# A written-out instruction order for all five engines, replaced by another one

## The chip, the cores and the metric

The kernel runs on one core of a Trainium2 chip. The metric is the device time of one execution in microseconds (us), the median of three runs. Besides the runs there is one execution recorded by the hardware profiler; every duration below is from its trace.

## The reference

The kernel computes one layer of an E-Branchformer (a speech encoder) and the gradients of its eight inputs from a given gradient of its output. Sizes: batch B = 2, T = 4000 tokens, D = 144 channels, taps K = 5, all in bf16.

```
xa   = layernorm(x)
q, k, v = split(xa @ w_qkv)
p    = softmax(q @ k^T * D**-0.5)            # 4000 x 4000 for each batch
glob = (p @ v) @ w_att_out
u, g = split(gelu(xa @ w_mlp_in))
gc   = depthwise_conv(layernorm(g), dw_csgu)  # 5 taps over time
loc  = (u * gc) @ w_mlp_out
m    = concat(glob, loc)
m    = m + depthwise_conv(m, dw_merge)
out  = x + m @ w_merge
return out, and the vjp of out for grad_out: dx and seven weight gradients
```

## The kernel before

**Tiling.** Each batch is cut into 32 tiles of 125 tokens. For each batch `phase_att` (L936) walks over its tiles and makes the forward and the backward of attention in one pass, while units of the local branch (`local_units`, L480: 5-tap convolution, GELU and their gradients) are worked in between. `Merge` (L1391) follows with the merge convolution, the output and dx, and `Final` (L1595) with the weight gradients. `Head` (L127) makes products of weights at the start.

**One tile of attention.** The names in italics are the short names of the text.

- *quad* (q0 to q3; L1028 and L1034): eight matmuls into PSUM (`ps`), 500 keys wide, for scores S of this tile and for dP of the tile before. L1034 adds the last 16 of the 144 channels.
- DVE takes a row statistic and copies (L1052), ACT makes the exponentials (L1060). P lies in `Pb`.
- SP issues the DMA transpose of P (`SX<-Pb`, L1064, *pt*). The two *y halves* (y0, y1; L1084) multiply the result with the layer-normed input into the one PSUM tile `yz`.
- dS is made from dP and P: ACT cast (L1073) and DVE product (L1075), or DVE alone (L1070). SP issues its DMA transpose in two halves (`SX<-SX`, L1256, *st0*, *st1*); the two *z halves* (z0, z1; L1131) multiply those.
- Small work on DVE, ACT and POOL after y (L1091 to L1113) and z (L1135) makes the operands of the next steps. SP issues the transposes of those too: `zt<-qz` (L1145, *zt*), `dhT<-dhr` of the local branch (L650, *dhT*), and `qt<-qz` (L1010, *jt*), which brings the query side of a later quad.
- *X groups* (x0 to x5; L1176): the gradients of keys and values, up to 16 matmuls each into a PSUM tile, which DVE adds to `acc` (L1180, L1182).
- *jm* (L988 to L992) is the projection of a later tile's queries; *t_unit*, *gc_unit*, *dgn*, *dug* are groups of the local branch (L597, L608, L623, L560).

The last two tiles of a batch use transposes on PE (L1121) in place of the DMA. With a `d` or `t` behind it, as in `st1t`, a name means the end of the first or the second batch.

**Fillers.** 126 matmuls of `warm` (L154) at the start and 50 (L1966) between the batches compute nothing that is used; they are part of PE's list like all others.

**The order.** The program is first emitted in the order of the code, and `Planner.grouped` (L898) collects it into 7014 groups: up to 16 matmuls of one PSUM tile (a quad is one group) on PE, one instruction on every other engine. `Planner.plan` (L924) then gives each engine the order that a table, `ORDER` (L723), holds as differences of group numbers, by chaining each instruction to the one before it without a semaphore:

```
    for e, order in ORDER.items():
        ...
        for g in order:
            for i in groups[g]["ins"]:
                if prev is not None:
                    self.tc.add_manual_dep(i, prev.name, ...NoSync...)
```

Each engine runs its list strictly in order: an instruction that waits for data holds all behind it. SP's list holds nearly all DMA issues, loads and stores as well as transposes. PE has 1799 groups, DVE 2394, ACT 1350, POOL 916 and SP 555.

**The ends.** At the end of the first batch and of the second, SP's list holds loads for the merge (`open_early`, L1402: `go_h`, `Yg`; `late_y`, L1427; `late_w`, L1443) beside the last transposes; `Hmm` (L1451, groups H0 to H15, L1459) needs them. The quads and outputs of the merge are L1556 to L1560. In the final stretch `dwm` (L1765) is a chain: a product into `pg` (L1773), five steps on DVE (L1780 to L1784), a transpose on PE (`fpt`, L1790), an ACT copy (L1793) and stores (L1786, L1795), once for 128 channels and once for 16.

Of the kernel before, what the change touches and what calls it, by code (L numbers as in the profile page):

```python
# [723 lines left out]
for _s in """  # L724
PE 10 1 1 1 1 1 1 1 1 1 1 1 1 1 1 1 1 1 1 1 1 1 1 1 1 1 1 1 1 1 1 185 -184 187 -186 1 1 1 1 1 1 1 1 1 1 1 1 1 1 1 1 173 2 11 -185 1 1 1 1 1 1 1 1 1 1
 198 -197 1 198 -197 1 1 1 1 1 1 195 -194 1 1 1 1 1 192 -191 1 1 1 1 1 1 1 1 1 1 1 1 209 2 62 -58 60 -57 -217 1 1 1 232 2 -233 1 1 1 1 1 1 276 -36 2
 24 -265 1 1 1 1 285 -21 2 2 71 14 -352 272 2 2 85 -83 2 2 83 -74 2 2 -294 1 295 2 -296 1 297 2 2 2 -302 304 5 -308 1 1 1 1 1 1 1 304 -303 1 305 -304
 1 311 -310 1 310 -309 1 309 10 35 11 -43 2 73 -70 6 91 -3 -86 22 69 -65 2 8 2 65 -62 2 13 9 73 -71 13 32 19 -16 4 10 23 -9 13 -17 29 -10 14 1 -7 24
 -6 34 -32 39 -25 32 -28 2 48 -46 3 5 14 6 14 2 18 -44 46 -14 1 17 10 18 -7 -2 10 9 -5 2 20 -13 2 9 6 1 24 -6 2 10 5 17 -7 -2 10 8 -4 8 2 2 11 -9 3 10
 1 -7 21 6 -4 38 -28 6 15 -2 14 4 -2 -6 12 5 11 -2 18 -12 1 13 4 13 5 13 -7 8 -10 20 -6 2 8 13 -8 6 6 12 -11 13 4 14 2 7 11 -2 14 3 -8 12 -11 22 -2 18  # L730
 -12 14 1 11 -25 30 -12 16 3 18 -7 -9 2 15 -11 1 16 -2 6 17 -15 7 6 18 -12 14 -13 31 -14 18 16 -7 -3 1 10 4 10 -8 12 8 2 18 2 -16 1 26 -7 10 4 17 -7
 -2 10 10 -6 2 8 14 -2 18 2 -14 16 -15 19 9 8 17 -7 -2 14 5 4 -13 18 7 -2 18 -12 1 13 4 6 3 2 19 -17 3 21 -17 8 14 6 -4 -6 14 14 -2 18 2 1 -15 1 24 -6
 36 -25 8 10 8 -10 14 5 4 5 3 2 16 -12 14 1 -14 24 -6 13 4 23 -9 2 12 1 -5 7 4 3 5 10 -2 18 -12 1 13 4 9 19 -9 2 12 -4 5 3 4 2 5 9 -6 2 8 -6 18 -11 14
 2 10 -6 33 -20 4 9 -2 14 9 -13 17 3 7 -2 18 -12 20 -19 21 4 9 19 -9 2 12 -4 7 4 2 3 9 -2 18 -12 1 13 4 6 13 17 -12 5 -2 10 9 -5 9 2 13 -2 6 12 -11 13
 5 -4 16 4 18 -7 -6 14 10 -20 14 2 22 -20 6 2 3 13 1 -7 18 2 11 -6 12 -16 28 12 -7 -2 14 2 -6 10 6 13 -2 -16 22 1 11 6 -4 15 18 -13 6 -2 14 -4 10 -4 8
 6 -5 13 -2 25 -19 1 24 -4 11 27 -7 -18 7 19 7 -17 14 18 -11 9 6 13 -12 14 4 6 5 3 21 -17 10 -8 2 4 10 10 -6 2 8 13 -8 6 6 12 -11 13 19 -18 4 16 25
 -18 9 2 12 7 -4 -7 20 2 16 -12 1 13 1 4 7 3 4 21 -7 -7 5 14 4 -8 12 14 -4 2 18 -12 1 13 13 -9 17 20 -9 2 12 -4 6 4 5 11 -6 3 7 12 -11 -7 24 -4 10 31
 -29 2 4 16 -11 9 14 5 -9 13 11 -8 5 7 12 8 -26 7 21 4 10 4 11 7 1 10 -24 4 14 27 -25 2 27 -21 2 5 8 7 21 -7 2 12 -11 38 -7 8 -24 5 28 -19 14 22 -13 3
 14 -9 10 18 -25 40 -22 2 1 12 -2 10 6 -2 6 4 4 -6 7 11 34 -32 1 46 -4 -6 2 2 10 -3 5 2 2 2 1 2 2 27 -25 27 -26 28 26 4 -28 32 -30 2 1 7 2 2 2 7 -5 2
 7 -3 4 4 -1 5 4 -6 4 4 -7 4 5 -1 4 -1 2 23 -1 4 1 -7 10 1 11 1 10 1 11 -41 52 12 -22 11 12 -61 12 59 12 -11 22 9 -80 89 -77 49 11 9 -58 12 63 9 9 -70  # L740
 44 -32 11 51 -21 25 -46 30 18 -9 -30 9 25 7 -3 5 2 -5 2 -24 9 20 -16 13 5 2 -5 2 200 1 1 1 1 1 1 -219 220 1 1 1 -182 -26 28 -26 207 1 1 1 1 1 -172 2
 171 1 1 1 1 -171 172 1 1 1 1 -174 175 1 1 1 -176 177 1 1 1 1 1 1 1 1 1 -175 2 4 2 168 1 1 1 1 1 1 -172 2 4 2 2 2 161 1 -160 2 1 169 -168 1 171 5 1 2
 1 4 3 -2 3 3 3 7 -28 50 -7 19 -18 2 1 6 1 2 1 23 -20 5 1 18 -16 1 21 3 1 -3 39 -32 1 41 -39 6 -5 8 4 42 -33 3 -2 3 33 1 16 -26 35 14 7 -17 28 -26 16
 -14 44 -40 14 2 8 14 6 1 11 2 4 6 5 8 2 7 5 4 4 2 3 -17 26 -2 20 2 -16 1 19 13 2 18 -9 2 12 -4 8 4 4 2 7 -5 3 18 2 10 -24 1 30 -13 17 14 2 12 6 -4 -7
 1 20 -7 5 6 12 -11 19 2 4 9 19 -7 -2 10 7 -3 7 14 -12 3 7 6 12 -11 13 10 6 -12 24 12 -7 -2 10 6 -2 6 5 11 4 1 -7 20 7 -5 16 -15 35 -15 8 8 -10 19 -5
 2 22 -15 2 17 -15 2 14 -11 4 25 -7 2 14 -13 19 23 -10 1 2 8 4 4 -2 6 5 11 -2 6 12 -11 17 -4 15 18 -7 -3 11 -10 19 -5 2 7 15 -13 7 4 20 2 -16 1 33 -14
 18 15 -7 -2 14 10 -8 -6 28 -10 8 6 1 11 2 4 9 22 -18 11 8 -14 24 -20 14 2 22 -20 6 2 3 13 -6 18 4 -15 21 -4 19 17 -12 5 -2 10 9 -5 9 2 13 -2 18 -12 1
# [1304 lines left out]
```

## Time and profile before

| | us |
|---|---|
| runs | 1248.24, 1252.67, 1252.02; median 1252.02 |
| profiled execution | 1248.45 |
| its span | 1246.7 |
| TensorE busy (PE) | 1202.6 |
| VectorE busy (DVE) | 1053.6 |
| ScalarE busy (ACT) | 739.3 |
| GpSimd busy (POOL) | 444.9 |

The span runs from the first to the last instruction of the trace; the profiled execution is 1.75 us longer. The mean granted clock of TensorE is 0.993. "PE" is matmuls, "PEld" weight loads that run beside them, "SPq" the time that SP's sequencer takes to issue a DMA. A wait is written with the engine and line that waits, and behind the arrow with what ended the wait. Roughly, the span is: head to 50 us, attention of the first batch to 550, the merge of the first batch to 650, attention of the second batch to 1150, the merge and the weight gradients to the end.

### The profile page before, as it was taken

The numbers are of one execution on the slowest core, as the hardware profiler recorded it, in microseconds if no ns is written. First come the engines' busy times: TensorE is split into PE (matmuls) and PEld (weight loads), VectorE is DVE, ScalarE is ACT, GpSimd is POOL, SyncE is SP. The second block draws the span as 40 slices with busy tenths as digits, with TensorE's granted clock in tenths as the row PEclk, the third lists the DMA queues.
The fourth block names the chain that finished last, engine by engine and source line by source line (L and its number), as shares of the span: only waits on it lengthen the run. The fifth ranks groups of instructions, "written<-read, shape, count | busy, mean of one in ns | idle before, by whom it ended". The sixth has DMA issues, their size and how long they took to land.

```text
span 1246.7 us, 38759 instructions
## 1 busy us (share of the span) xinstructions
PE 1202.6 (96%) x15890; PEld 947.8 (76%) x15890; DVE 1053.6 (85%) x2862; ACT 739.3 (59%) x1183; POOL 444.9 (36%) x920
## 2 busy tenths in 40 slices
PE   9999999999999999999999999999999999999997
PEld 7667777777777777789876777777777777677996
DVE  8688989898989888879769898989888989877665
ACT  5866555656565656544746656666656666554273
POOL 8444333433333333213534433333334333222020
PEclk9899999999999999999999999999999999999998
DMA  3579999898989999985249889999898999999332
GB/s 106 121 133 155 161 154 162 155 166 156 169 153 165 150 160 160 163 201 156 66 103 158 159 162 161 156 166 152 147 174 157 159 159 170 169 171 188 95 101 69
DMA packets 638399, 186.52 MB, mean 150 GB/s; under 512 B 621025, under 2 KB 633164, under 8 KB 638214
## 3 DMA queue, kind: packets, MB, share of 16 engines
q1 hardware_dynamic: 616664, 176.66, 79.6%
q10 hardware_dynamic: 21348, 7.13, 2.9%
q8 instruction: 124, 2.03, 0.7%
q14 instruction: 55, 0.45, 0.1%
q0 software_dynamic: 208, 0.25, 0.1%
HBM read 20.82 MB, written 14.22 MB: 28 GB/s over the span
## 4 chain that ended last, share of the span: by engine, by line
PE 62%; DVE 15%; DMA 14%; ACT 6%; issue 2%; SPq 1%; POOL 1%; ACTq 0%; DVEq 0%; POOLq 0%
PE X L1176 14%; PE ps L1028 11%; PE yz L1131 8%; DMA SX<-SX 6%; PE yz L1084 5%; PE ps L1034 5%; DMA SX<-Pb 4%; DVE Pb L1052 4%; PE Hps L1459 3%; PE po L1556 3%; ACT Pb L1060 2%; DVE acc L1182 2%; DVE SX L1075 2%; DMA qt<-qz 1%; PE warm L154 1%
## 5 line engine op out<-in xcount | busy, mean ns | idle before, releaser
L1052 DVE TENSOR_SCALAR_CACHE_REDUCE Pb<-ps 125x1000 bf16<-125x1000 f32 x256 | 306.0, 1196 | 68.7 <-PE ps L1034 66.1
L1060 ACT ACTIVATE Pb<-Pb,nm 125x1000 bf16<-125x1000 bf16 x256 | 277.4, 1127 | 120.8 <-DVE nm L1054 119.9
L1176 PE MATMUL X<-SX 125*128 125x144 bf16 x2048 | 294.5, 227 | 2.0 <-DVE acc L1180 0.7
L1176 PE MATMUL X<-SX,Pb 125*128 125x144 bf16 x2048 | 293.8, 226 | 0.0
L1073 ACT CAST SX<-ps 125x1000 bf16<-125x1000 f32 x189 | 187.9, 994 | 161.5 <-PE ps L1034 159.9
L1028 PE MATMUL ps<-xaT_m,qt 128*128 128x500 bf16 x1024 | 262.2, 376 | 8.7 <-DVE Pb L1052 5.2
L1182 DVE TENSOR_TENSOR acc<-X,acc 125x432 f32<-125x432 f32 x372 | 201.2, 550 | 30.6 <-PE X L1176 29.6
L1176 PEld LDWEIGHTS <-SX 125*128 125x128 bf16 x2048 | 197.3, 97 | 28.9 <-issue 27.7
L1176 PEld LDWEIGHTS <-Pb 125*128 125x128 bf16 x2048 | 200.2, 98 | 3.7 <-issue 3.1
L1131 PE MATMUL yz<-xa_aug,SX 125*128 125x144 bf16 x2048 | 151.6, 229 | 11.6 <-DMA SX<-SX 9.5
L1084 PE MATMUL yz<-xa_aug,SX 125*128 125x145 bf16 x2048 | 145.7, 227 | 4.1 <-DMA SX<-Pb 4.1
L1131 PEld LDWEIGHTS <-SX 125*128 125x128 bf16 x2048 | 132.8, 98 | 20.7 <-DMA SX<-SX 13.8
L1028 PEld LDWEIGHTS <-qt 128*128 128x128 bf16 x1024 | 91.0, 98 | 71.1 <-issue 8.4
L1084 PEld LDWEIGHTS <-SX 125*128 125x128 bf16 x2048 | 132.6, 98 | 6.7 <-DMA SX<-Pb 5.6
L1075 DVE TENSOR_TENSOR SX<-SX,Pb 125x1024 bf16<-125x1024 bf16 x189 | 131.2, 698 | 7.4 <-ACT SX L1073 5.0
L1034 PEld LDWEIGHTS <-qt 16*128 16x128 bf16 x1024 | 26.6, 91 | 111.3 <-issue 111.3
L1034 PE MATMUL ps<-XR,qt 16*128 16x500 bf16 x1016 | 102.1, 382 | 0.0
L1070 DVE TENSOR_TENSOR SX<-ps,Pb 125x1000 bf16<-125x1000 f32 x67 | 80.1, 1195 | 2.5 <-PE ps L1034 1.9
L638 POOL TENSOR_SCALAR l_w<-gdr,nc,c 125x144 f32<-125x144 bf16 x64 | 30.5, 481 | 94.2 <-DVE c L636 84.5
L533 POOL TENSOR_SCALAR l_a<-l_sq 125x576 bf16<-125x576 bf16 x32 | 23.2, 725 | 111.7 <-ACT l_sq L531 107.2
L1109 POOL TENSOR_SCALAR SX<-qz,rl 125x144 bf16<-125x144 bf16 x62 | 25.1, 405 | 95.0 <-DVE rl L1091 84.3
L1004 POOL COPY qz<-qz 125x64 bf16<-125x64 bf16 (+1 forms) x124 | 34.0, 292 | 67.9 <-ACT qz L994 67.1
(475 smaller groups left out, 2141.6 us busy)
## 6 DMA issues: line engine op xcount, KB each, us to landing
go_h<-in_grad_out_dram SPq DMA_DIRECT2D x4, 567.0 KB
Yg<-ug_d SPq DMA_DIRECT2D x4, 567.0 KB
Yn_d<-yn ACTq DMA_DIRECT2D x64, 35.2 KB
Zn_d<-qz ACTq DMA_DIRECT2D x64, 35.2 KB
ug_d<-ugr ACTq DMA_DIRECT2D x32, 70.3 KB
SX<-in_x_dram SPq DMA_DIRECT2D x16, 140.6 KB
out_dram<-Pb SPq DMA_DIRECT2D x16, 140.6 KB
out_dram<-SX SPq DMA_DIRECT2D x16, 140.6 KB
```

Source lines behind the costliest of these rows:

```text
L1028: mm = nc.tensor.matmul(pp[r // 2][:, r % 2, 0:CH], QT[i][:, 3 * h, :], xaTm[:, c * CH:(c + 1) * CH], start=True, stop=False)
L1034: nc.tensor.matmul(pp[r // 2][:, r % 2, 0:CH], QT[i][rs, 1 + h, :], xr, start=False, stop=True)
L1052: nc.vector.tensor_scalar(pv(Pbuf, i % NPB, c2), src, -1.0, 3.0e38, op0=ALU.mult, op1=ALU.min, accum_out=NM[i][:, c2:c2 + 1])
L1060: nc.scalar.activation(v, v, ACT.Exp, bias=NM[i][:, 4:5], scale=-1.0)
L1070: nc.vector.tensor_tensor(pv(Sbuf, i % NDB, c2), src, pv(Pbuf, i % NPB, c2), op=ALU.mult)
L1073: nc.scalar.copy(pv(Sbuf, i % NDB, c2), src)
L1075: nc.vector.tensor_tensor(sc, sc, pchunk(i % NPB, c2), op=ALU.mult)
L1084: nc.tensor.matmul(Y, PT[0:PB, j, :], xaa[:, j, 0:D + 1], start=(j == 0), stop=(j == NB - 1))
L1131: nc.tensor.matmul(Z, ST[0:PB, j, :], xaa[:, j, 0:D], start=(j == 0), stop=(j == NB - 1))
L1176: nc.tensor.matmul(X[:, jj, :], l, r, start=(n_ == 0), stop=(n_ == len(ops) - 1))
L1182: nc.vector.tensor_tensor(av, X[0:PB, 0:nj, :], av, op=ALU.add)
L1459: nc.tensor.matmul(H[a // 6][0:rows, a // 3 % 2, (a % 3) * D:(a % 3 + 1) * D], lhs, self.src[h][:, 2 + j, :], start=(j == 0 and a % 3 == 0 ...
```

## The change

The table `ORDER` is replaced by another, made from durations that were read from a trace. The groups, their instructions, operands, buffers and semaphores are the same; only the order in each engine's list differs.

```diff
 ORDER = {}
 for _s in """
-PE 10 1 1 1 1 1 1 1 1 1 1 1 1 1 1 1 1 1 1 1 1 1 1 1 1 1 1 1 1 1 1 185 -184 187 -186 1 1 1 1 1 1 1 1 1 1 1 1 1 1 1 1 173 2 11 -185 1 1 1 1 1 1 1 1 1 1
...
+PE 10 1 1 1 1 1 1 1 1 1 1 1 1 1 1 1 1 1 1 1 1 1 1 1 1 1 1 1 1 1 1 1 1 1 1 1 1 1 1 1 1 1 1 1 1 1 1 1 1 1 1 1 1 1 1 1 1 1 1 1 1 1 1 1 1 1 1 1 1 1 146
...
 """.strip().replace("\n ", " ").split("\n"):
```

(The lines of all five engines change in this way.) Decoded, the two tables compare like this. In attention most groups stand within a place or two of where they stood:

| engine | entries | at the same place | median of places moved | most |
|---|---|---|---|---|
| PE | 1799 | 789 | 1 | 49 |
| DVE | 2394 | 463 | 2 | 103 |
| ACT | 1350 | 206 | 2 | 52 |
| POOL | 916 | 190 | 2 | 43 |
| SP | 555 | 129 | 1 | 94 |

Places of which the text speaks, with the start that each group has in the trace of before:

| place | list before | list of the change |
|---|---|---|
| PE, head | 31 fillers, `hps` (7.83), ..., first quad (19.55) at place 99 | 70 fillers, `hps`, ..., first quad at place 114 |
| PE, attention (one example) | jm 1107.01, z0 1109.17, q1 1110.20, dgn 1111.46, x0 1111.78, x1 1112.53, q2 1113.28 | jm, q1, dgn, x0, x1, z0, q2 with x2 ahead of it |
| SP, attention (one example) | pt 1110.20, jt 1115.15, st0 1116.48, st1, pt, dhT 1129.80, zt 1131.71 | pt, jt, zt, st0, st1, pt, dhT |
| PE, 576 to 612 | H groups, then 50 fillers among transposes of the second batch's input | up to 34 of the fillers stand earlier, among the H groups |
| SP, 1133 to 1165 | st0t 1132.99, zt 1134.85, two loads, st1t 1138.14, then 14 loads and more | st0t, eight loads, zt, six loads, st1t |
| POOL, 1135 to 1143 | clears of `Yg` at 1141.85 and 1142.52 behind L1111 to L1113 | the same clears 14 and 15 places earlier |
| PE, tail | `pg` of 16 channels 1230.09, quads of the output, transposes and products 1233.46 to 1235.76 (six groups), last `pg` 1235.99 | last `pg` ahead of those six groups |

In the second row from the top the count of X groups that stand earlier and of z, y and q groups that stand later is the main regularity of PE's list; in SP's list it is a zt that stands ahead of an st (42 times in the two attention stretches).

6 lines of the change are left out of this document (3 added, 3 removed), and 277 rows, old and new, of the table ORDER.

## The prediction

> **What bounds the kernel now.** I read the page's engine totals first, then its chain of waits, then the stretches of the span, then what TensorE waited for.
>
> ```profile
> span 1246.7 us, 38759 instructions
> PE 1202.6 (96%) x15890; PEld 947.8 (76%) x15890; DVE 1053.6 (85%) x2862; ACT 739.3 (59%) x1183; POOL 444.9 (36%) x920
> PE 62%; DVE 15%; DMA 14%; ACT 6%; issue 2%; SPq 1%; POOL 1%; ACTq 0%; DVEq 0%; POOLq 0%
> ```
>
> TensorE is busy for 1202.6 of 1246.7 us, so at most 44.1 us of recorded idle time can go; no matmul is removed. The chain that ends last runs through PE for 62%, and through DVE and DMA for 15% and 14%: where PE is not the one that works, it waits for an eviction or a transpose. The profiled execution took 1248.45 us, 1.75 us more than its span. It lies near the lowest of the three runs (1248.24) and 3.57 us under their median (1252.02).
>
> ```profile
> 0.00:25.00 25.00, 23.57 (x185) 19.66 (x185) 20.64 (x85) 13.12 (x35) 21.66 (x48) 1.00 0.43 113
> 25.00:50.00 25.00, 24.94 (x245) 15.15 (x243) 17.25 (x32) 19.87 (x40) 11.76 (x49) 0.89 0.39 96
> 100.00:550.00 450.00, 439.63 (x5846) 337.20 (x5846) 399.13 (x1023) 272.52 (x412) 158.58 (x330) 1.00 0.94 160
> 550.00:600.00 50.00, 49.95 (x802) 49.67 (x800) 42.02 (x182) 24.38 (x35) 15.89 (x21) 1.00 0.56 146
> 600.00:650.00 50.00, 47.25 (x618) 40.35 (x616) 35.76 (x88) 28.82 (x54) 22.53 (x38) 1.00 0.38 92
> 650.00:1150.00 500.00, 483.87 (x6394) 371.19 (x6392) 438.53 (x1116) 303.87 (x457) 177.41 (x373) 1.00 0.95 162
> 1225.00:1246.70 21.70, 13.41 (x152) 9.91 (x150) 13.82 (x71) 4.41 (x17) 1.93 (x2) 0.82 0.26 72
> ```
>
> The columns are the stretch, its length, busy time of PE, PE weight load, DVE, ACT and POOL, PE's granted clock, the DMA share and GB/s. The two attention stretches hold 10.4 and 16.1 us of PE's idle time, and their DMA share is 0.94 and 0.95. The last stretch holds 8.3 us, 600 to 650 holds 2.75. What the change can win is therefore in attention and in the last 21.7 us.
>
> ```profile
> PE yz L1131 <- DMA SX<-SX: 9.5, 11, 2.6
> PE ps L1028 <- DVE Pb L1052: 5.2, 11, 1.7
> PE fpt L1790 <- DVE Pb L1788: 4.6, 2, 2.4
> PE yz L1084 <- DMA SX<-Pb: 4.1, 7, 0.9
> PE ps L1028 <- DMA qt<-qz: 3.1, 5, 0.9
> ```
>
> Waits of PE: total, times, longest. Three of the five are DMA transposes that land late: dS^T before a z half (9.5), P^T before a y half (4.1) and q^T before a score quad (3.1), together **16.7 us**.
>
> **The change part by part.** Work and buffers stay; only who stands ahead of whom in each of the five queues moves. So nothing is added to the 1202.6 us, and each part is worth only what it does to waits.
>
> *Attention, PE's queue.* Comparing the two lists, I see one systematic move: X groups (L1176) go ahead of y, z and q groups. Of the 118 z groups 50 stand behind at least 0.3 us more PE work than before, of the 119 y groups 36, of the 228 quads 42; the mean is 0.47 us for z0, 0.86 for z1, 0.33 for y and 0.37 for q0.
>
> ```profile
> 1107.19 0.47 PE L992 MATMUL pj<-VUT,goT 128*125 128x144 bf16 x5
> 1109.17 1.19 PE L1131 MATMUL yz<-xa_aug,SX 125*128 125x144 bf16 x16 [1.50 <-DMA SX<-SX]
> 1110.20 1.01 PE L1028 MATMUL ps<-xaT_m,qt 128*128 128x500 bf16 x4
> 1111.46 0.30 PE L623 MATMUL pd<-eb,gT 128*128 128x68 bf16 x4
> 1111.78 0.22 PE L1176 MATMUL X<-SX 125*128 125x144 bf16 x1
> 1113.28 1.01 PE L1028 MATMUL ps<-xaT_m,qt 128*128 128x500 bf16 x4
> 1090.60 1.19 PE L1131 MATMUL yz<-xa_aug,SX 125*128 125x144 bf16 x16 [2.63 <-DMA SX<-SX]
> ```
>
> At 1109.17 a z half waits 1.50 us for its transpose. In the new list the quad and the three groups behind it (1110.20 to the next quad at 1113.28: 3.08 us) stand ahead of it, which is more than the wait. At 1090.60, the longest wait (2.63), PE's list is unchanged. The X groups that move forward are ready: of 154 that go ahead by over 0.3 us one alone would wait, for 0.2 us, by the ends of its producers in this trace.
>
> *Attention, SP's queue.* Every transpose is issued by SP, in order, and an issue is not short:
>
> ```profile
> L1145 SPq DMA_TRANSPOSE zt<-qz x60: 1177/1254/2346, 83.6 to 1134.9; - x60
> L650 SPq DMA_TRANSPOSE dhT<-dhr x32: 1222/1282/2625, 151.4 to 1129.8; - x32
> L1256 SPq DMA_TRANSPOSE SX<-SX x124: 1558/2324/4082, 49.9 to 1138.1; - x124
> L1064 SPq DMA_TRANSPOSE SX<-Pb x62: 4724/5220/6641, 36.1 to 1124.3; - x62
> ```
>
> These are ns (min, median, max). The new list puts a zt ahead of a dS^T transpose 42 times, at a median of 1.25 us of SP each. I walked SP's new list with the readiness and the issue durations of this trace: the dS^T transposes are issued 0.7 us later on average (P^T 0.13), because a zt or dhT now stands in front of them. That takes back what the X groups give: set against PE's new list, the lead of a landing over its z half changes by -0.09 (z0) and +0.21 (z1) us, over y0 by +0.13, over a quad by +0.18. Some leads get longer (1109.17: 3.08 more work less an issue 1.23 later, enough for its 1.50), others fall short: 27 of some 246 landings, by 28.0 us together, of which 5.8 are one case below. Readiness is itself a result of the old order, so for an item moved forward this walk shows it too late: the 28.0 is an upper end. **I take 0** for attention: the mean lead hardly moves. Bounds: -16.7 (all three waits gone) to +22.2 (28.0 less 5.8, each a wait).
>
> The Trainium skill, page "DMA: Bandwidth & Descriptors", section "Issuing engines are not separate DMA queues", says that the sequencer's time to start a DMA is usually small beside the DMA itself. By that rule a zt ahead of a dS^T would cost nothing, the shortfalls would mostly vanish, and the sum would go to its lower bound. The rows speak against it here: 1.25 and 2.32 us of SP per issue are not small beside waits of 0.9 to 2.6.
>
> *DVE, ACT and POOL in attention.* Median moves of two places, in queues that are 0.89 or less busy. DVE's score statistics are the one wait of PE on them (5.2 us in the rows above). A promoted DVE item that isn't ready holds what is behind it, and the quads wait for that; a quad that comes 0.37 us later gives the same back. I take 0; bounds -5.2 and +5.2, the same row both ways.
>
> *Head.* All 126 warm fillers stay, but 70 instead of 31 stand ahead of the first real group.
>
> ```profile
> 7.83 0.22 PE L194 MATMUL hps<-ident,Pb 128*128 128x128 bf16 x1
> 9.03 2.31 PE L154 MATMUL warm<-SX 128*125 128x290 bf16 x17
> 11.18 0.41 PE L220 MATMUL hps<-SX 128*128 128x144 bf16 x4
> 19.55 0.59 PE L1028 MATMUL ps<-xaT_m,qt 128*128 128x500 bf16 x2
> ```
>
> A filler takes (11.18 - 9.03) / 17 = 0.126 us, so the group of 7.83 comes 39 x 0.126 = 4.9 us later. The first quad (19.55) has 15 more places ahead, all fillers: +1.9 us. By 44 us both lists have done the same work, and PE has no idle time in 25 to 50, so the delay is paid only as far as later steps hang on the first quad. I take +1.9, bounds 0 and +4.9.
>
> *Between the batches.* Up to 34 of the 50 second fillers go from 595-612 into 576-594, where PE had no idle time, and H groups and transposes come 3 to 4 us later. The cover is then missing where PE waits for the layer norm:
>
> ```profile
> 594.75 1.02 PE L1966 MATMUL warm<-VUT,ident 128*125 128x288 bf16 x7
> 606.80 0.60 PE L410 MATMUL pt<-ident,go_r 125*80 125x125 bf16 x8 [1.28 <-DVE R L411]
> ```
>
> At the head's 0.126 us each, 34 of them are 4.3 us: an upper end if all that they hid comes out. The H groups that fill in instead are the same work, and the wait that shows is 1.28, so I take +1.0, bounds 0 and +4.3.
>
> *End of batch two.* The last dS^T transpose goes 15 places back on SP, behind loads for the merge.
>
> ```profile
> 1138.14 2.84 SPq L1256 DMA_TRANSPOSE SX<-SX  x1
> 1144.62 1.19 PE L1131 MATMUL yz<-xa_aug,SX 125*128 125x144 bf16 x16
> ```
>
> SP's walk issues it 11.5 us later, its z half has 3.9 us more work ahead and 1.8 us of slack: the 5.8 us short. Part of the walk's delay is a load that waits for a POOL memset, which the new POOL list does 15 places earlier; without it the shortfall is near 0. I take half, +2.9; bounds 0 and +5.8. The Trainium skill, page "TensorE: Matmul & The Clock Gate", section "HAM oscillation", says that PE gaps beyond about 3.4 us throttle the clock; an estimate by it is some 1.7 us more if the wait comes out whole. The sum leaves it out.
>
> *Tail.*
>
> ```profile
> 1233.46 0.17 PE L1790 MATMUL fpt<-ident,Pb 16*5 16x16 bf16 x1
> 1233.56 0.49 PE L1615 MATMUL fpt<-ident,Pb 128*128 128x128 bf16 x4
> 1233.99 0.28 PE L1556 MATMUL po<-SX 128*125 128x144 bf16 x1
> 1234.55 0.51 PE L1625 MATMUL fpt<-goT,Pb 128*128 128x144 bf16 x4
> 1235.99 0.79 PE L1773 MATMUL pg<-Pb,xaT_m 128*128 128x432 bf16 x4
> 1239.15 0.27 PE L1790 MATMUL fpt<-ident,Pb 128*5 128x128 bf16 x1 [2.38 <-DVE Pb L1788]
> ```
>
> The last dependent chain is pg at 1235.99, five DVE steps, a transpose, pg again, DVE again, and the last store. Its list is unchanged, but it begins six PE places earlier: the transposes and products of 1233.46 to 1233.99 (0.53 us), of 1234.55 and of the same line just ahead of pg (some 0.44 each, their 0.51 less the overlap) now come behind it. That is -1.4 us, bounds -8.3 (the stretch's idle time) and 0.
>
> **Sum** against 1248.45: 0 + 0 + 1.9 + 1.0 + 2.9 - 1.4 = +4.4, so 1252.9; rounded, **1253 us**, beside the median of 1252.02. A difference under about 0.5% (6.3 us) can't be told from no change here.
>
> **The rivals.** *Faster: X groups cover the transposes.* The transposes' producers are moved forward as well, the shortfalls vanish, and the 16.7 us of DMA waits go: 1248.45 - 16.7 + 4.4 = 1236. For it: the move of X groups is aimed at exactly those waits, and X groups are ready. Against: SP's own issues come 0.7 us later, and DMA is already 0.94 busy. *Slower: SP's order decides.* The zt and dhT issues ahead of dS^T make z halves late; half of the 22.2 us bound is 11.1: 1248.45 + 4.4 + 11.1 = 1264; all of it is 1275. It decides once more than some 6 us of the 22.2 turn into waits. For it: 42 x 1.25 us; against: z halves stand 0.47 to 0.86 us later too. *The order is not kept*: each engine runs its queue in program order, so I give this nothing of its own.
>
> **How the numbers follow.** Forecast 0.37 (1246 to 1258), faster rival 0.28, slower rival 0.35. The range takes in the slower rival's whole size and the faster rival with most of the tail's bound (1236 - 6.9 = 1229): 1230 to 1275. Faster by over 0.5% 0.28, within 0.37, slower 0.35.
>
> **What would show it.** PE's waits for dS^T and P^T should stay near 13.6 us with other places; the wait at 1109 should be gone. A total under 5 is the faster rival, over 20 the slower. The first quad should start near 21.5 us, the last z half behind its transpose near 1150 should wait up to 5.8 us, and the last pg chain should begin 1.4 us nearer to the end. I am wrong if DVE or POOL becomes what PE waits for in attention, or if the busy time of PE itself moves.

## The result and the profile after

The changed kernel takes **1242.17 us** (median of seven runs, 1238.75 to 1245.96), the kernel before 1248.85 us beside it (seven runs, 1248.24 to 1252.67). The ratio is **0.9941, with an interval of 0.9922 to 0.9959**: some 7 us, or 0.59%, faster. The forecast was no measurable difference, 1253 us. The profiled execution of the changed kernel took 1242.5 us.

The first rows are from the page of the changed kernel: its span, the engine totals, and the chain that ended last by engine.

```profile
span 1240.7 us, 38869 instructions
PE 1198.4 (97%) x15890; PEld 950.0 (77%) x15890; DVE 1058.6 (85%) x2862; ACT 740.1 (60%) x1183; POOL 461.4 (37%) x920
PE 61%; DVE 16%; DMA 12%; ACT 4%; POOL 4%; issue 3%; ACTq 0%; SPq 0%; DVEq 0%; POOLq 0%
```

PE's matmuls are as many as before, the span is 6.0 us shorter, and the chain of waits has the same make: PE for 61%, then DVE and DMA. Nothing else became the bound. The stretches of the span show where PE's idle time went, and a row of 5 us shows the place that the end of the second batch pays for. The columns are those of the prediction's rows.

```profile
100.00:550.00 450.00, 442.28 (x5914) 342.36 (x5912) 400.30 (x1032) 272.52 (x410) 163.87 (x331) 1.00 0.98 166
550.00:600.00 50.00, 46.44 (x700) 45.74 (x699) 47.47 (x192) 27.32 (x45) 24.25 (x30) 0.96 0.30 84
650.00:1150.00 500.00, 482.44 (x6344) 369.48 (x6342) 438.80 (x1105) 301.23 (x452) 185.81 (x371) 1.00 0.96 163
1140.00:1145.00 5.00, 1.14 (x17) 0.79 (x15) 1.25 (x3) 0.99 (x1) 0.00 (x0) 1.00 1.22 175
1225.00:1240.70 15.70, 10.11 (x124) 7.70 (x121) 10.16 (x53) 2.45 (x11) 0.00 (x0) 0.89 0.21 59
```

The first batch's attention (100 to 550) now has 7.7 us of PE idle instead of 10.4. The merge behind it (550 to 600) has 3.6 instead of 0.05, and in the five microseconds from 1140 on PE works for 1.14. The last stretch has 5.6 us of PE idle where before had 8.3. So the change wins and loses at the same time, by stage. What PE waited for, over the whole span (total, times, longest):

```profile
PE yz L1085 <- DMA SX<-Pb: 6.6, 9, 1.8
PE yz L1132 <- DMA SX<-SX: 6.2, 8, 1.4
PE ps L1029 <- DVE Pb L1053: 4.7, 14, 0.8
PE pt L410 <- DVE R L450: 3.3, 1, 3.3
PE Hps L1460 <- issue: 2.9, 1, 2.9
PE fpt L1791 <- DVE Pb L1789: 2.8, 2, 2.1
PE Hps L1460 <- DMA Pb<-in_x_dram: 2.1, 1, 2.1
```

(Lines stand one further down than before.) The waits for P^T, dS^T and q^T, 16.7 us before, are 12.8 here: neither gone nor grown. Three waits are new, of 3.3, 2.9 and 2.1 us, all in the two merges.

How far the changed kernel is ahead of the one before is read best from when both start the same group. These leads are the starts of the same groups in the two traces, one taken from the other (us ahead of before; the column head is the start in the trace of before):

| place | 91 | 508 | 619 | 688 | 1069 | 1123 | H0 (1153) | H15 (1195) | last `pg` of 128 channels |
|---|---|---|---|---|---|---|---|---|---|
| lead | 6.8 | 13.4 | 5.3 | 3.7 | 4.2 | 7.6 | 9.8 | 1.3 | 4.2 |

The first batch's attention gains 6.6, the stretch between the batches loses what was won there, and the stretch from 1069 to 1123 gains 3.4. From 1123 to H15 the end of the second batch loses 6.3. Two things make this loss look larger than it is: H0 stands earlier in the new list, so its 9.8 is in part its new place, and some work that came behind H15 now comes ahead of it. At the end of the span the lead is 6.0, so from 1123 on 1.6 is lost in all. The 6.8 at 91 are partly chance, as the section on the hardware shows.

### The profile page after: what moved, and what is told of

Same layout as the page of the kernel before. It is cut to its first block, busy times and chain, and to the rows that moved or that the text cites. A ratio compares the mean times of both kernels' runs of the same rounds, so it can differ in the third digit from the quotient of the medians.

```text
span 1240.7 us, 38869 instructions
## 1 busy us (share of the span) xinstructions
PE 1198.4 (97%) x15890; PEld 950.0 (77%) x15890; DVE 1058.6 (85%) x2862; ACT 740.1 (60%) x1183; POOL 461.4 (37%) x920
## 4 chain that ended last, share of the span: by engine, by line
PE 61%; DVE 16%; DMA 12%; ACT 4%; POOL 4%; issue 3%; ACTq 0%; SPq 0%; DVEq 0%; POOLq 0%
PE X L1177 14%; PE ps L1029 11%; PE yz L1132 7%; PE yz L1085 7%; DMA SX<-Pb 6%; DMA SX<-SX 5%; PE ps L1035 4%; DVE Pb L1053 4%; PE po L1557 3%; DVE acc L1183 2%; PE Hps L1460 2%; ACT Pb L1061 1%; DVE SX L1076 1%; PE warm L154 1%; DVE SX L1071 1%
## 5 line engine op out<-in xcount | busy, mean ns | idle before, releaser
L1183 DVE TENSOR_TENSOR acc<-X,acc 125x432 f32<-125x432 f32 (+1 forms) x372 | 200.2, 550 | 15.0 <-PE X L1177 13.3
L1076 DVE TENSOR_TENSOR SX<-SX,Pb 125x1024 bf16<-125x1024 bf16 x189 | 134.3, 715 | 10.4 <-ACT SX L1074 6.9
L1460 PE MATMUL Hps<-Yg,go_h 125*128 125x144 bf16 x640 | 54.1, 229 | 5.0 <-issue 2.9
L1005 POOL COPY qz<-qz 125x48 bf16<-125x48 bf16 (+1 forms) x124 | 34.9, 298 | 58.6 <-ACT qz L995 40.0
```

What stands on the lines that cost most here:

```text
L1076: nc.vector.tensor_tensor(sc, sc, pchunk(i % NPB, c2), op=ALU.mult)
L1183: nc.vector.tensor_tensor(av, X[0:PB, 0:nj, :], av, op=ALU.add)
L1460: nc.tensor.matmul(H[a // 6][0:rows, a // 3 % 2, (a % 3) * D:(a % 3 + 1) * D], lhs, self.src[h][:, 2 + j, :], start=(j == 0 and a % 3 == 0 ...
```

## The experiments

All kernels here compute the whole reference; only the order differs. Fourteen take the order of the change in some stretches and the order of before in the others. `OLD` and `NEW` are the two decoded tables; each engine's old list is cut at counts (the groups that had started before a given time in the trace of before), and each piece takes its groups in the order of one of the tables:

```diff
-ORDER = {}
+CUT = {...}; PICK = "NOOOO"; ORDER = {}
+for _e in OLD:
+    _c = [0] + CUT[_e] + [len(OLD[_e])]
+    ORDER[_e] = []
+    for _i, _p in enumerate(PICK):
+        _in = set(OLD[_e][_c[_i]:_c[_i + 1]])
+        ORDER[_e] += [_x for _x in (NEW if _p == "N" else OLD)[_e] if _x in _in]
```

Both tables stand in these kernels, so their lines stand further down: a quad is L1186, y L1242, z L1289, X L1334. Each result is a median, beside the kernel before on the same chip, with the ratio and its interval. The theory was at first that of the prediction (attention gives nothing, the ends cost); the rival was that attention gains and the two ends give it back.

**1 to 4: one stretch at a time.** Cuts at 100, 535, 655 and 1130 us: head, first attention, between the batches, second attention, end.

```diff
+CUT = {"PE": [248, 772, 1019, 1590], "DVE": [190, 1023, 1278, 2178],
+       "Activation": [142, 616, 724, 1236], "Pool": [137, 457, 531, 884],
+       "SP": [58, 211, 298, 467]}
+PICK = "NOOOO"   # 1: head        2: "ONOOO"   3: "OONOO"   4: "NNONN"
```

Experiment 1, the new head alone:

> The new lists for what started before 100 us in the trace of before, the old lists for all the rest. In the two traces the same quads start 6.8 us earlier at 91 us, and before loses about 5 us there to a lower granted clock (0.50 in 45 to 50, 0.66 in 75 to 80). Theory of stages (each stretch gains or loses by itself): 6 to 7 us faster than before, some 1242, and no clock under 0.9 ahead of 100 us. Rival (the gain of the head is lost again later, since attention is bound by its own transposes): under 2 us faster. My prediction's term for the head was 1.9 us slower.

Measured: 1246.7 beside 1248.82; 0.9992 [0.9976, 1.0009]. The head is worth -1.0 us by the ratio, give or take 2.

Experiment 2, the new order in the first attention alone:

> The new lists only for 100 to 535 us (attention of the first batch). The same quads gain another 6 to 7 us there between the two traces. Theory of stages: 5 to 7 us faster than before, some 1243. Rival (the lead of attention is only the head's, carried on, or noise of one trace): within 2 us of before. My prediction's term was 0.

Measured: 1241.05 beside 1248.82; 0.9935 [0.9912, 0.9958]. This one stretch gives **8.1 us**, as much as the whole change. The traces agree. From the quad that starts at 100.00 us in the trace of before to the one at 518.34, the nine traces with the new order in this stretch (experiments 2, 4, 7 to 11 and 16, and the change) pull ahead of before by 3.6 to 8.3 us, with a median of 7.0. The six others with the old order of all engines there fall behind it by 0.6 to 2.8.

Experiment 3, the new order between the batches alone:

> The new lists only for 535 to 655 us (end of the first batch's attention, merge, start of the second). There the new order gives back 7 to 8 us between the two traces, with waits of PE of 2.1 us (H0 for a load) and 3.3 us (a transpose for DVE) and a clock of 0.66, 0.56 and 0.76 in three stretches of 5 us. Theory of stages: 6 to 8 us slower than before, some 1256, with both waits. Rival (the loss only shows because PE arrives earlier than the loads and the layer norm, which don't come earlier; with the old attention ahead nothing is lost): within 2 us of before.

Measured: 1254.16 beside 1248.82; **1.0041 [1.0023, 1.0059]**, 5.1 us slower. Its waits of PE from 530 to 665, and a stretch of its span:

```profile
PE pt L410 <- DVE R L450: 3.3, 1, 3.3
PE X L1334 <- DMA zt<-qz: 3.1, 1, 3.1
```

```profile
600.00:615.00 15.00, 11.67 (x142) 11.28 (x140) 11.18 (x26) 9.59 (x18) 9.35 (x12) 0.78 0.10 30
```

The first wait is the same as in the changed kernel: the transposes of the second batch's input now meet an unfinished layer norm, since the fillers that covered it went by earlier. The second is an X group behind a zt. SP issues that zt 0.7 us later than before (544.0 against 543.3), and PE is ready for the matmul that needs it 3.7 us earlier (546.5 against 550.2). And PE's clock falls to 0.78 for 15 us.

Experiment 4, the whole change except between the batches:

> The new lists everywhere but in 535 to 655 us, where the old ones stand. Theory of stages: the loss of 7 to 8 us goes, 1234 to 1236, which would be faster than both kernels. Rival (loads and layer norm between the batches set a time of their own): as the changed kernel, 1240 to 1243.

Measured: 1243.68 beside 1248.82; 0.9955 [0.9938, 0.9972]. This is the changed kernel's time within the intervals, although experiment 3 says that the omitted part costs 5.1. The stretches **do not add**.

**5 and 6: the first attention by queue.** SP's list alone, and the four engines' lists alone, each from 100 to 535 us. (PE's new list alone, or with SP's, can't run: the engines would wait for each other in a circle.) This tells whether SP's order or PE's gives the 8.1.

```diff
+PICK = {"PE": "OOOOO", "DVE": "OOOOO", "Activation": "OOOOO", "Pool": "OOOOO", "SP": "ONOOO"}  # 5
+PICK = {"PE": "ONOOO", "DVE": "ONOOO", "Activation": "ONOOO", "Pool": "ONOOO", "SP": "OOOOO"}  # 6
```

> Of the second run's edit only SP's list: the new order of DMA issues for 100 to 535 us, PE, DVE, ACT and POOL as before. The second run was 0.65% (some 8 us) faster than before. Theory A (X groups in front of z, y and q cover the transposes, which is PE's list with its helpers): SP's list alone gains nothing, or loses, since my walk has the dS^T issues 0.7 us later: 0 to 8 us slower than before. Theory B (zt and dhT issued earlier is what helps): 5 to 8 us faster. Theory C (each alone is worth nothing, they fit only together): both halves within 2 us of before, or slower.

Measured: 1256.41 beside 1249.52; **1.0059 [1.004, 1.0078]**, 7.3 us slower.

> The other half: new lists of PE, DVE, ACT and POOL for 100 to 535 us, SP's list as before. Theory A: 5 to 10 us faster than before, more than the second run if SP's new list costs something, and PE's waits for DMA transposes there well under the 6.2 us of before. Theory B: within 2 us of before or slower. Theory C: within 2 us of before, or slower.

Measured: 1245.34 beside 1249.52; 0.9965 [0.9945, 0.9985], 4.4 us faster.

The waits of PE for transposes from 100 to 530: first before, then SP's list alone (5), the engines' lists alone (6), both together (2), and the change:

```profile
PE ps L1028 <- DMA qt<-qz: 2.5, 4, 0.9
PE yz L1084 <- DMA SX<-Pb: 2.0, 4, 0.7
PE yz L1131 <- DMA SX<-SX: 1.7, 4, 0.7
```

```profile
PE yz L1289 <- DMA SX<-SX: 6.8, 10, 1.8
PE ps L1186 <- DMA qt<-qz: 4.5, 3, 2.5
PE yz L1242 <- DMA SX<-Pb: 0.6, 2, 0.4
```

```profile
PE ps L1186 <- DMA qt<-qz: 4.2, 4, 2.2
PE yz L1242 <- DMA SX<-Pb: 1.1, 1, 1.1
PE yz L1289 <- DMA SX<-SX: 1.0, 1, 1.0
```

```profile
PE yz L1289 <- DMA SX<-SX: 3.6, 4, 2.1
PE yz L1242 <- DMA SX<-Pb: 0.5, 1, 0.5
```

```profile
PE yz L1132 <- DMA SX<-SX: 1.1, 2, 0.7
PE yz L1085 <- DMA SX<-Pb: 0.7, 2, 0.5
```

Added up these are 6.2 us before, 11.9 with SP's list alone, 6.3 with the engines' lists alone, 4.1 with both, and 1.8 in the changed kernel. One trace can't bear much, since the same order gives other waits in another execution: over all kept traces the sum is 6.2 to 9.3 in the seven with the old order of all engines in this stretch, and 1.8 to 5.5 in the nine with the new. SP's new list alone makes dS^T late (6.8), as the prediction's walk said. The wait that goes only when the lists go **together** is that for q^T: 2.5 to 3.6 us with the old order, 4.5 with SP's list alone, 4.2 with the engines' alone, and not listed in any of the nine traces with the new order. The wait for P^T falls as well (1.6 to 2.8 with the old order, 0.4 to 1.7 with the new). That for dS^T does not: 1.7 to 3.7 with the old order, 1.1 to 5.0 with the new.

SP's own idle time shows why the lists need each other. Ahead of the 26 zt issues of the stretch SP stands idle for 1.8 us before, and for 8.5 when its new list runs alone: it comes to a zt whose data are not there yet, and holds all that is behind it. With the engines' new lists beside it (experiment 2) this is 2.4. In the second attention the same three figures are 3.8, 10.4 and 4.8 (before, experiments 15 and 13). The gain of the pair (8.1) is more than the engines' 4.4 and SP's loss of 7.3 put together, by 11.0 us.

A sum over all matmuls from 100 to 535 gives the same picture. Take the distance from each matmul's start to the next one's, beyond the shortest that five traces show for that matmul: together this is 19.3 us before, 12.6 in the changed kernel, 14.7 in experiment 2, 26.6 with SP alone and 16.1 with the engines alone. Nearly all that changes lies in idle times over 0.15 us, which the profile lists as waits (12.0, 6.5, 7.5, 17.8 and 10.4 of these sums).

**7 and 8: two single entries of the changed kernel.** In 7 the last dS^T transpose, st1t (group 6384), goes right behind st0t (6352) in SP's list, ahead of all the loads; in 8 the fillers that were moved go back ahead of the transposes that wait 3.3.

```diff
+_l = ORDER["SP"]; _l.remove(6384); _l.insert(_l.index(6352) + 1, 6384)   # 7
+_w = list(range(3636, 3666))                                              # 8
+_l = [_x for _x in ORDER["PE"] if _x not in _w]
+_i = _l.index(3486); ORDER["PE"] = _l[:_i] + _w + _l[_i:]
```

> The changed kernel with one entry of SP's list put back: the last dS^T transpose of the second batch (st1t) goes right behind st0t again, ahead of the merge loads. In the changed kernel PE is busy for 1.14 of the 5 us from 1140 and its clock is 0.66 in the next 5. My prediction's step (up to 5.8 us, 2.9 taken, and some 1.7 of clock beside it): 3 to 6 us faster than the changed kernel, some 1237 to 1239. Rival (the merge's loads, which then come later, set the end of the stretch, as in the old order where nothing is lost there): within 1.5 us of the changed kernel.

Measured: 1247.17 beside 1249.52; 0.9986 [0.9965, 1.0007]. By the two ratios that is 5.6 us **slower** than the changed kernel, though it mends the wait that it was aimed at. Its waits of PE from 1130 on, and the five microseconds behind them:

```profile
PE X L1329 <- DMA zt<-qz: 4.3, 1, 4.3
PE Hps L1612 <- DMA go_h<-in_grad_out_dram: 2.9, 1, 2.9
```

```profile
1145.00:1150.00 5.00, 1.63 (x13) 1.34 (x13) 1.12 (x2) 0.99 (x1) 0.00 (x0) 0.50 0.94 256
```

SP came to the loads and zt only 8.95 us after it began with the two transposes. Each issue took 1.9 us; between them SP waited 5.07 us for st1t's data, which before and in the changed kernel other issues fill:

```profile
1126.95 8.95 SPq L1409 DMA_TRANSPOSE SX<-SX  x2
```

So what now stands behind st1t is late in its place: zt by 4.3, the merge's load by 2.9. The wait moved, and the granted clock of the next stretch is 0.50.

> The changed kernel with the 30 fillers that it has among the H groups (places 846 to 894 of PE's list) put just ahead of the transposes of grad_out (L410), where PE waits 3.33 us for DVE in the changed kernel and the clock falls to 0.56 and 0.76. If the cover was lost, as my prediction's upper end has it (4.3 us): 3 to 6 us faster than the changed kernel, and no clock under 0.9 in 590 to 610. Rival (the fillers do hide something at 570 to 585, evictions of the transposed pieces, so that the wait only moves): within 1.5 us of it.

Measured: 1244.6 beside 1249.52; 0.9951 [0.9931, 0.9971], the changed kernel's time within the intervals. The wait of 3.3 is gone from 525 to 615, and these stand there:

```profile
PE X L1330 <- DMA zt<-qz: 2.7, 1, 2.7
PE pm L1541 <- ACT SX L1537: 2.5, 2, 2.2
```

Only the second is new. A wait for that zt of 2.9 and 3.2 us stands also in the traces of experiments 7 and 10, whose lists are those of the change in this stretch, where the change's own trace has 1.1.

**9 to 12: finer stretches.** 9 takes the new order only from 100 to 535, from 1080 to 1130 and from 1200 on; 10 takes the change with the old order from 1130 to 1200; 11 the change with the old order from 535 to 573; 12 the new order from 1080 to 1130 alone.

```diff
+CUT = {"PE": [248, 772, 1533, 1590, 1734], "DVE": [190, 1023, 2091, 2178, 2310],
+       "Activation": [142, 616, 1188, 1236, 1296], "Pool": [137, 457, 854, 884, 909],
+       "SP": [58, 211, 449, 467, 519]}; PICK = "ONONON"                       # 9
+CUT = {"PE": [1590, 1734], "DVE": [2178, 2310], "Activation": [1236, 1296],
+       "Pool": [884, 909], "SP": [467, 519]}; PICK = "NON"                    # 10
+CUT = {"PE": [772, 839], "DVE": [1023, 1091], "Activation": [616, 637],
+       "Pool": [457, 474], "SP": [211, 259]}; PICK = "NON"                    # 11
+CUT = {"PE": [1533, 1590], "DVE": [2091, 2178], "Activation": [1188, 1236],
+       "Pool": [854, 884], "SP": [449, 467]}; PICK = "ONO"                    # 12
```

> New lists of all engines where the runs so far show a gain (100 to 535, 1080 to 1130 and from 1200 us on, by the trace of before), old lists elsewhere. If the stretches add: 8 us from the first (the second run), some 2 to 3 from the z halves at 1090 and 1109, some 2 from the tail: 1236 to 1239 against 1249, faster than both kernels. Rival (stretches don't add, as the head's lead and the fourth run showed): as the second run, 1240 to 1242.

Measured: 1242.45 beside 1249.19; 0.9949 [0.9927, 0.9971]. The stretches that looked best, taken together, give 6.4 us, no more than experiment 2 alone.

> The changed kernel with the old lists of all engines in 1130 to 1200 us (the last transposes, the merge's loads and the H groups of the second batch). One entry alone put back (st1t) was no gain, since PE then waited 4.3 us for a zt behind the same loads. Theory (SP's order of transposes and loads and PE's early H groups make the loss together): 4 to 6 us faster than the changed kernel, 1236 to 1238. Rival (what is lost there is a time that the loads set): as the changed kernel.

Measured: **1237.66** beside 1249.19; **0.9905 [0.9887, 0.9923]**, 11.9 us faster than before and by the medians 4.5 us faster than the changed kernel, whose interval it only just touches. Its row for the place at which the changed kernel's PE worked 1.14 us, and PE's wait for the merge's loads from 1130 to 1200:

```profile
1140.00:1145.00 5.00, 3.76 (x63) 3.63 (x62) 2.69 (x10) 3.01 (x5) 0.00 (x0) 1.00 0.86 235
```

```profile
PE Hps L1617 <- DMA Yg<-ug_d: 1.2, 1, 1.2
```

PE works 3.76 us there instead of 1.14, and the H groups wait 1.2 instead of 2.9. How much that is worth in time, the leads tell only roughly. At the quad that starts at 1123.18 in the trace of before, experiment 10 is 10.8 us ahead and the change 7.6, though their lists are the same up to there: two executions of one order differ by that much. From that quad to the end of the span the four traces with the new order in this stretch (the change, 4, 8 and 11) lose 1.5 to 3.0 us on before, and the two with the old order from 1130 to 1200 and the new behind it (9 and 10) gain 0.5 and 0.8. By these the stretch costs 2 to 4 us.

> The changed kernel with the old lists of all engines in 535 to 573 us, which puts the first H groups of the first batch behind the y halves again and the loads for them in the old order. In the changed kernel PE waits 1.1 us there for a zt, 2.1 us for a load ahead of H0, and its clock is 0.66 in 540 to 545. Theory (early H0 costs that): 3 to 5 us faster than the changed kernel at 573, 1238 to 1240 at the end. Rival (PE only meets the later wait for the layer norm, 3.3 us at 593, that much longer): as the changed kernel.

Measured: 1241.73 beside 1249.19; 0.9941 [0.9919, 0.9962], the changed kernel's time. The wait of the input's transposes is 1.7 instead of 3.3, but it is 1.7 in experiment 10 too, which leaves this stretch as in the change; so the edit needn't be the cause. A wait of 3.1 for an ACT step (`pm`) is new.

> The new lists for 1080 to 1130 us alone, where my prediction saw a z half that waits 1.50 us at 1109 covered by 3.08 us of other work, and one that waits 2.63 us at 1090 with PE's list unchanged and its transpose issued 1.24 us earlier. By those two leads: 1.5 + 1.2 us, so 2 to 3 us faster than before, at the edge of what can be told; the wait at 1109 gone in the profile, that at 1090 near 1.4. Rival (the waits move to y halves, as between 655 and 1080): no difference, and y waits of 1 to 2 us.

Measured: 1246.22 beside 1249.19; 0.9975 [0.9959, 0.999]. These 50 us alone give 3.1.

**13 to 16: the second attention, and old order at both ends.** 13 is the new order from 655 to 1080, 14 the same without SP, 15 on SP alone; 16 is the change with the old order from 535 to 655 and from 1130 on.

```diff
+CUT = {"PE": [1019, 1533], "DVE": [1278, 2091], "Activation": [724, 1188],
+       "Pool": [531, 854], "SP": [298, 449]}; PICK = "ONO"                    # 13 to 15
+    ... (NEW if _p == "N" and _e != "SP" else OLD)                             # 14
+    ... (NEW if _p == "N" and _e == "SP" else OLD)                             # 15
+CUT = {"PE": [772, 1019, 1590], "DVE": [1023, 1278, 2178], "Activation": [616, 724, 1236],
+       "Pool": [457, 531, 884], "SP": [211, 298, 467]}; PICK = "NONO"         # 16
```

> The new lists of all engines for 655 to 1080 us alone (attention of the second batch without its last tiles). By the two traces, where PE's lead shrinks by 2 to 3 us there: 0 to 3 us slower than before. Rival (the lead shrinks only because a lead is lost in attention anyway; by itself the stretch gains as the first batch's does): 4 to 8 us faster.

Measured: 1249.49 beside 1249.18; 0.9998 [0.9979, 1.0017].

> The new lists of PE, DVE, ACT and POOL for 655 to 1080 us, SP's list as before. If SP's new order (zt and dhT ahead of dS^T) spoils what the X groups ahead of z, y and q win: 3 to 6 us faster than before, as the sixth run (4.4) in the first batch. If the engines' new lists have nothing to win there: within 2 us of before.

Measured: 1247.89 beside 1249.18; 0.9983 [0.9965, 1.0002], 2.1 us faster by the ratio, at the edge of what can be told.

> SP's new list alone for 655 to 1080 us. As the fifth run in the first batch (7.3 us slower, z halves waiting 6.8 us for dS^T): 4 to 8 us slower than before. If SP's list is harmless here: within 2 us of before.

Measured: 1260.84 beside 1249.18; **1.0087 [1.0056, 1.0118]**, 10.9 us slower.

The waits of PE for transposes from 650 to 1075 in experiment 15:

```profile
PE yz L1242 <- DMA SX<-Pb: 6.8, 5, 2.6
PE yz L1289 <- DMA SX<-SX: 5.8, 8, 2.5
PE ps L1186 <- DMA qt<-qz: 2.1, 3, 1.4
```

SP's list alone is as bad here as in the first batch (14.7 us of these waits), and the engines' lists take it back again. But the pair leaves the waits where they were: 2.8 to 6.3 us in the eight traces with the new order here, 3.1 to 7.4 in the eight with the old. The wait that the pair removed in the first batch, that for q^T, is at most 0.7 us here with the old order, so there was little to win; that this is the reason is a reading, not a test.

> The new lists up to 535 and from 655 to 1130 us, the old ones between the batches and from 1130 us on. Against the tenth run (old lists in 1130 to 1200 only, 11.9 us faster than before) it takes the new lists between the batches away, which alone cost 5.1 us, and the tail's, which show no gain between the traces. If the loss between the batches counts once the end keeps the lead: 3 to 5 us faster than the tenth run, some 1233 us. Rival (the second batch's attention gives a longer lead back, as the fourth run showed): as the tenth run, 1237 to 1239.

Measured: 1236.15 beside 1249.18; 0.9896 [0.9863, 0.9928], 13.0 us faster than before, and the same as experiment 10 within the intervals. These two are the fastest kernels of the study.

By the ratios the single stretches are: head -1.0, first attention -8.1, between +5.1, second attention -0.2, 1080 to 1130 -3.1; the end from 1130 to 1200 +4.5 from experiment 10. They predict experiment 16 well (-1.0 - 8.1 - 0.2 - 3.1 = -12.4; measured -13.0), but experiment 4 badly (-7.4 for the change less 5.1 = -12.5; measured -5.6) and experiment 9 badly (-8.1 - 3.1 = -11.2, its tail left aside; measured -6.4). Leaving out either loss alone between 535 and 655 (4, 8, 11) gave nothing, leaving out the end gave 4.5. Experiment 16 says the same of the end: it differs from experiment 4 from 1130 us on alone, and is 7.4 us faster by the ratios, with intervals that don't touch.

Why the loss between the batches appears when its stretch is changed alone, and doesn't go when it is taken out, the leads show in good part. From the quad at 518.34 to the one at 650.00 the four traces with the whole new order there (the change, 3, 7 and 10) lose 3.2 to 8.8 us on before, and the eleven with the old one 0.4 to 1.6. So experiment 4 does keep what it was meant to keep. In the next 50 us, up to the quad at 699.12, the three in which the new second attention follows the old order (4, 13 and 16) lose 2.0 to 4.0, and the three in which it follows the new one (the change, 7 and 10) 0.3 to 0.6. Experiments 4, 11 and 16 have one wait at this seam that the change has not, a y half behind a DVE step of the local branch; here it is from experiment 4:

```profile
PE yz L1242 <- DVE st L548: 2.3, 1, 2.3
```

An order suits the order ahead of it, and a seam between two orders costs time of its own. The -0.2 of the second attention alone (experiment 13) holds such a loss too. What is left of the 5.1 is within the intervals of experiments 4 and 16. Why experiment 9 gives so little **stays open**.

## Why the prediction was wrong

It said that the time would stay where it was, and the time fell by 0.59%, beyond what it called measurable. By its steps:

*Attention, "I take 0: the mean lead hardly moves".* **This step failed.** The first attention gives -8.1 (experiment 2), the second -0.2 (13), the 50 us from 1080 on -3.1 (12): some -11 together where 0 stood, if they add, which they don't in experiment 9 (-6.4); the whole change is -7.4. The working walked SP's new list with the ready times of the old order, and judged PE's list by the same old times. Each walk by itself was right in sign: SP's list alone costs 7.3 and 10.9 us (experiments 5 and 15), 18 for both batches, near the walk's upper end of 22.2. But readiness is a result of all five lists. With the engines' new lists in place the producers come earlier, as SP's idle time ahead of a zt shows (8.5 us alone, 2.4 with them), and SP's new places fit; the pair gains in the first batch and breaks even in the second. The prediction named that flaw ("this walk shows it too late") and used it only to bound the loss; it had to be used for the value, too, since an item that becomes ready earlier can turn a loss into a gain. The mean of the lead was also the wrong thing to look at: what the pair removes in every trace is a few waits for q^T (2.5 us in 4 places before), and these hardly show in a mean over all quads.

*The three waits as measure of the gain.* Their total went from 16.7 to 12.8 us, neither under 5 nor over 20, so by the prediction's own sign neither rival was right. The gain was real nevertheless: within 100 to 530 the same waits went from 6.2 to 1.8. A total over the span mixes a stage that won with one that lost. The waits for dS^T and P^T alone, which the prediction put near 13.6 us, are 12.8; what is gone from the list is q^T, 3.1 before.

*The single places in attention were right.* The wait at 1109 is gone, and the longest wait, whose place in PE's list is unchanged, shrank from 2.63 to 0.51 us, which the prediction had not expected. The two z halves in the changed kernel:

```profile
1082.02 1.19 PE L1132 MATMUL yz<-xa_aug,SX 125*128 125x144 bf16 x16 [0.51 <-DMA SX<-SX]
1102.85 1.18 PE L1132 MATMUL yz<-xa_aug,SX 125*128 125x144 bf16 x16
```

*Head, +1.9.* Mis-sized, and off the path: alone it is worth -1.0 with an interval of -3.0 to +1.1 (experiment 1). The first quad did come later, at 20.16 instead of 19.55 us, by 0.6 and not 1.9, and nothing later hung on it: at the quad at 100.00 the five traces with the new head and no clock drop at 45 us (see the section on the hardware) are 4.6 to 5.9 us ahead of before, and the eight such traces with the old head 0.7 to 3.6.

```profile
20.16 0.59 PE L1029 MATMUL ps<-xaT_m,qt 128*128 128x500 bf16 x2
```

*Between the batches, +1.0.* The mechanism was right, the size too small: +5.1 alone (experiment 3), above the bound of 4.3. PE waits 3.33 us where the fillers are gone, as the prediction said, and also for a zt that PE reaches before it has landed, and it runs with a clock of 0.78; it had counted neither.

```profile
596.68 1.00 PE L410 MATMUL pt<-ident,go_r 125*80 125x125 bf16 x8 [3.33 <-DVE R L450]
```

*End of batch two, +2.9, bounds 0 and +5.8.* Right in mechanism, and by the medians in size: the old order in this stretch is 4.5 us faster (experiment 10). The prediction saw one item of it, st1t, whose issue on SP took twice as long as before, 5.71 us against 2.84. The z half behind it then waits 1.00, and H0 ahead of it 2.87.

```profile
1136.94 5.71 SPq L1257 DMA_TRANSPOSE SX<-SX  x1
1143.46 0.54 PE L1460 MATMUL Hps<-Yg,go_h 125*128 125x144 bf16 x6 [2.87 <-issue]
1144.99 1.31 PE L1132 MATMUL yz<-xa_aug,SX 125*128 125x144 bf16 x10 [1.00 <-DMA SX<-SX]
```

The wait of H0 is put down to "issue", so the trace names no releaser for it; that it waits for loads isn't shown. Mending st1t alone made the kernel slower (experiment 7): the cost belongs to the order of the whole stretch, not to that entry. After such a gap the clock is down as well, which the sum had left aside; 5 us at 0.66 are 1.7 lost, the figure that the prediction had named beside its sum:

```profile
1145.00:1150.00 5.00, 5.00 (x56) 5.00 (x57) 1.05 (x2) 0.37 (x1) 0.57 (x1) 0.66 0.72 170
```

*Tail, -1.4.* Right in mechanism, not shown in time. From the last `pg` of 128 channels to the end it is 8.92 us (1240.7 - 1231.78) instead of 10.71 (1246.7 - 1235.99), 1.8 us less, and the waits of the transposes for DVE are 2.8 instead of 4.6.

```profile
1231.78 0.53 PE L1774 MATMUL pg<-Pb,xaT_m 128*128 128x432 bf16 x2
```

No run has the new tail alone. Experiments 9 and 10, with the old order from 1130 to 1200 and the new tail, gain 0.5 and 0.8 us on before from the quad at 1123.18 to the end; the ten with the old order from 1130 to the end gain 0.9 in the median (-1.8 to 1.8). So no gain of the tail is seen there.

*DVE, ACT and POOL, 0.* Neither DVE nor POOL became what PE waits for in attention (DVE's statistics 5.2 before, 4.7 after). Their new lists together can't run without PE's, since the engines would then wait for each other in a circle. That they count is seen only in that the four engines' lists together made room for SP's. The other sign of being wrong, a change of PE's own busy time, did come: 1202.6 before, 1198.4 after, much of it probably the clock drop at 45 us.

*The rivals.* The faster one was right in sign, within its first part: "the transposes' producers are moved forward as well". Its price of 16.7 was too high: the waits for q^T went, those for P^T fell in the first batch alone, and those for dS^T stayed. The slower one, SP's order, is real alone and is undone by the other lists. With the attention term at its measured value the prediction's own sum would have been 1241.5 (1252.9 less 11.4), about what was measured, though in part by luck: those three don't add in every experiment, and the errors of its head and between terms nearly cancel. That the stated range (1230 to 1275) holds the measured time is due to its width.

## What to carry to other kernels

When an order is judged from a trace, walk all queues together and let each item's ready time follow from the new places; a list walked with the old ready times finds the losses of that list and none of the gains of the pair. Look at the landings with the least slack, stage by stage, and not at the mean lead or at a total over the span. Test a plan stage by stage, and expect seams: a stretch in its old order can spoil the start of a new one behind it. Here the order of before in the 70 us from the last of attention into the merge, with the new order everywhere else, was 4.5 us better by the medians than the plan as a whole, while mending one entry of that stretch made the kernel slower. And compare more than two traces: one order gave sums of the same waits from 1.8 to 5.5 us in nine traces.

## What the runs showed of the hardware

**A clock drop that comes and goes.** From 45 to 50 us the trace of before shows a granted clock of 0.50 with PE busy all the time; the changed kernel's shows 1.00. That looks like a gain of the new head, and it is none: of the 18 profiles, before and experiments 7, 8, 15 and 16 have 0.50 there and the other 13 have 1.00, with old and new heads on both sides. The stretch before, and in experiment 3, which has the same head list, and then a quad of each:

```profile
45.00:50.00 5.00, 5.00 (x17) 1.21 (x15) 3.98 (x6) 2.56 (x7) 0.00 (x0) 0.50 0.01 3
```

```profile
45.00:50.00 5.00, 5.00 (x43) 2.69 (x43) 4.33 (x8) 4.12 (x10) 0.81 (x2) 1.00 0.03 7
```

```profile
74.68 1.42 PE L1028 MATMUL ps<-xaT_m,qt 128*128 128x500 bf16 x4 [1.73 <-DVE Pb L1052]
```

```profile
71.62 1.01 PE L1186 MATMUL ps<-xaT_m,qt 128*128 128x500 bf16 x4 [1.73 <-DVE Pb L1210]
```

The same quad, with the same wait of 1.73, starts 3.06 us earlier where the drop is missing. So about 3 of the 6.8 us of lead at 91 in the table of leads are chance, and the 4.2 us by which PE's busy time is shorter there (1202.6 less 1198.4) will hold much of it; how much wasn't separated. The Trainium skill, page "TensorE: Matmul & The Clock Gate", section "What's actually happening", says that the gate watches a window of some 3.4 us that runs free of the kernel's start, so that the phase differs from run to run. The traces agree with a window of that size: apart from the last one at each kernel's end, every stretch of half clock in the 18 traces lasts 3.41, 6.83 or 10.24 us. The one at 45 us in the trace of before lasts 6.83, and half of that is near the 3.06. The drop falls 45 us into a kernel with PE recorded as busy; what sets it off there isn't shown.

**Where an issue stands on SP is worth microseconds.** SP's list alone, with the same transfers and the same bytes, made the kernel 7.3 us slower in one batch and 10.9 in the other. The Trainium skill, page "DMA: Bandwidth & Descriptors", section "Issuing engines are not separate DMA queues", calls the sequencer's time to start a DMA usually small beside the DMA itself. The prediction said that the trace spoke against that here. The runs show the price of the order, but not that sentence's comparison, since the traces have no landing times of these transposes; part of the price is SP standing idle ahead of a zt, 8.5 us against 1.8 before. An issue's length isn't fixed either: that of st1t took 5.71 us in the changed kernel, behind a run of loads, 2.84 before, and 1.89 in experiment 7, which puts it ahead of the loads. That fits loads that lengthen it; the mechanism isn't shown.
